# Retention attention followed by top-1 expert routing: a third buffer for transposed keys, and the gate weights by one transfer and eight copies

## The chip, the cores and the metric

The kernel runs on one core of a Trainium2 chip. The metric is the time of one execution on the device in microseconds (us), as the median of several runs. The engines named here are TensorE (PE; its weight loads are listed apart as PEld), VectorE (DVE), ScalarE (ACT), GpSimd (POOL) and SyncE (SP), which only issues transfers. Each works through its own instructions in order and waits on semaphores for the others. SBUF is the memory on the chip that they share, PSUM the one that TensorE writes its results to.

## The reference

Attention of the retention kind (a decay in place of a softmax) over 8 batches, 8 heads, 576 positions and heads of 64, and then a layer of 8 experts in which each of the 4608 tokens goes to the one expert with the highest logit.

```python
def _attn_ref(q, k, v):                       # each (8, 8, 576, 64)
    scores = scale * np.matmul(q, k.transpose(0, 1, 3, 2))
    gamma = 1.0 - 2.0 ** (-5.0 - np.arange(H))
    Dmat = np.where(rel >= 0, gamma[:, None, None] ** rel[None, :, :], 0.0)   # rel = i - j
    return np.matmul(scores * Dmat[None], v)

def _moe_ref(x, w_gate, w1, w2):              # x (4608, 512), w_gate (512, 8), w1 (8, 512, 1024), w2 (8, 1024, 512)
    logits = x @ w_gate
    expert_idx = np.argmax(logits, axis=1)
    ...                                       # softmax of the logits; gate_w = the winner's share
    for e in range(E):
        mask = expert_idx == e
        ye = np.maximum(x[mask] @ w1[e], 0.0) @ w2[e]
        out[mask] = gate_w[mask, None] * ye
    return out
```

`x` is the attention's output with the heads side by side.

## The kernel before

Attention goes through 40 blocks: for each of 8 batches four blocks of 128 positions (c = 0 to 3) and a remainder of 64 (c = 4, so blocks 4, 9, 14, ...). Block i+1 finds a running state `se` of what came before it. Keys and queries are scaled on GpSimd by their share of the decay (`scale_k`, `scale_q`), transposed on TensorE (`stage_TK`, `stage_TQ`) and copied from PSUM by ScalarE into `kT` and `qT`. For a remainder the 64 queries and 64 keys share one tile, so its `kT` serves as queries too and is read until the end of its own iteration. Pools hand out a fixed number of buffers for each tag (`bufs`) in turn: a tile waits until all readers of the one that had its buffer are done.

```python
    wkp = p1.enter_context(tc.tile_pool(name="wk", bufs=2))
    wk3 = p1.enter_context(tc.tile_pool(name="wk3", bufs=3))
# ... cut ...
    def stage_TK(i):
        if i >= NB:
            return
        kk = kks[i]
        pst = psw.tile([P, 512], F32, tag="W", name="psk")
        for p in range(NP):
            tr(pst[:, p * P:(p + 1) * P], kk[:, 2 * p:2 * p + 2, :].rearrange("p h d -> p (h d)"), ident[:, :])
        kT = wkp.tile([P, NP, P], F32, tag="kT")
        mark["kT"] = nc.scalar.copy(out=kT[:, :, :].rearrange("p a t -> p (a t)"), in_=pst[:, :])
        kTs[i] = kT
# ... cut: stage_S adds a block's keys and values to the state ("pss"); stage_SC makes the scores ...
    def stage_SC(i):
        if i >= NB:
            return
        b, c = blocks[i]
        kT = kTs.pop(i)
        sc = wk1.tile([P, 2, NP, P], F32, tag="sc")
        scs[i] = sc
        if c < NCH:
            qT = qTs[b]
            for p in range(NP):
                for u in range(2):
                    for j in range(2):
                        r = slice(j * DH, (j + 1) * DH)
                        mm(pssc[u * DH:(u + 1) * DH, j, p * P + u * DH:(p + 1) * P], kT[r, p, u * DH:(u + 1) * DH],
                           qT[r, p, c * P + u * DH:(c + 1) * P], True, True)
            mark["sc"] = nc.vector.tensor_tensor(
                out=sc[:, :, :, :].rearrange("p j a i -> p (j a) i"),
                in0=pssc[:, :, :].rearrange("p j (a i) -> p (j a) i", i=P),
                in1=mask[:, :].unsqueeze(1).to_broadcast([P, 2 * NP, P]), op=ALU.mult)
        else:
            qTs[(b, "r")] = kT
# ... cut: the remainder's own scores; stage_AV multiplies scores by values into "psx" ...
    def stage_IN(i):

        b, c = blocks[i]
        if c < NCH:
            mark["xT"] = nc.vector.tensor_copy(
                out=xTs[b][:, c, :].rearrange("p (w t) -> p w t", w=2), in_=psx[:, :, 0:2 * P])
            xbs[i] = wkb.tile([P, 2, 2 * P], BF16, tag="xb", name="xb")
            nc.scalar.copy(out=xbs[i][:, :, :], in_=psx[:, :, 0:2 * P])
        else:
            # ... cut ...
            se, qT = sts.pop((b, c)), qTs.pop((b, "r"))
            # ... cut: matmuls into psx that read the remainder's kT (here qT) ...
            xo = wk1.tile([P, 256], F32, tag="xo", name="xo")
            nc.scalar.copy(out=xo[:, :], in_=psx[:, 1, 256:512])
            xTs[(b, "r")] = wk1.tile([P, 256], F32, tag="xTr", name="xTr")
            mark["xT"] = nc.vector.tensor_tensor(out=xTs[(b, "r")][:, :], in0=psx[:, 0, 256:512], in1=xo[:, :],
                                                 op=ALU.add)
            xbs[i] = wkb.tile([P, 256], BF16, tag="xb", name="xb")
            nc.scalar.copy(out=xbs[i][:, :], in_=xTs[(b, "r")][:, :])
```

Before the blocks begin, SyncE issues the first loads of queries, keys and values (`load_q`, `load_k`, `load_v`, up to block 4), and then the gate weights. These are wanted in a form that fits the transposed output: `wgp` has, for each pair of heads and two variants, 64 rows of one head above 64 of another, and 8 of 32 columns filled. Eight transfers bring the pieces. The first use of `wgp` is `stage_L1` of the first batch, in the iteration of block 5.

```python
    wgp = attc.tile([P, 2, NP, 32], F32, name="wgp")
    nc.vector.memset(wgp[:, :, :, :], 0.0)
    wg4 = moe_w_gate.rearrange("(a u d) e -> u d a e", u=4, d=DH)
    for j in range(2):
        for w in range(2):
            nc.sync.dma_start(out=wgp[j * DH:(j + 1) * DH, 0, 2 * w:2 * w + 2, 0:E], in_=wg4[(3 * w, 2 - w)[j]])
            nc.sync.dma_start(out=wgp[j * DH:(j + 1) * DH, 1, w:NP:2, 0:E], in_=wg4[2 * w + (j ^ w)])
```

The loop over the blocks: GpSimd scales ahead by three blocks, keys are transposed ahead by two, scores are made ahead by one, and key and value loads are issued six blocks ahead, each after a mark of the pace. The constants of the routing are made on GpSimd in the iteration of block 3.

```python
    scale_k(0, nc.vector)
    stage_TK(0)
    for p in range(NP):
        scale_q(0, p, nc.vector)
        stage_TQ(0, p)
    scale_k(1)
    scale_k(2)
    stage_TK(1)
    stage_SC(0)
    stage_S(0)
    load_k(5)
    load_v(5)
# ... cut ...
    for i, (b, c) in enumerate(blocks):
        if i == 3:
            make_routing()

        if c > 0 and b + 1 < B:
            scale_q(b + 1, c - 1)
        scale_k(i + 3)
        fetch(early.get(i, 0))
        load_k(i + 6, mark.get("sc"))
        stage_TK(i + 2)
        if c > 0 and b + 1 < B:
            stage_TQ(b + 1, c - 1)
        if c == 1 and b > 0:
            stage_L2(b - 1)
        if i > 1:
            stage_R(i - 2)
        if c in (1, 3) and b + 2 < B:
            load_q(b + 2, c // 2, mark.get("kT"))
        stage_S(i + 1)
        stage_AV(i)
        if c == 0 and b > 0:
            stage_L1(b - 1)
        stage_IN(i)
        stage_SC(i + 1)
        load_v(i + 6, mark.get("xT"))
        if (b, c) == (B // 2, 1):
            rf = route_first()
        if rf is not None:
            steps(rf, 1.9)
```

`stage_R` writes a block's output as rows for the expert layer, `stage_L1` and `stage_L2` make a batch's logits, `route_first` is the routing of the first half of the tokens, a few VectorE steps in each iteration from batch 4 on. After the loop come the experts: rows gathered by token, transposed, multiplied by w1, through the ReLU, by w2, scaled, and scattered to the output.

Of the kernel before, what the change touches and what calls it, by code (L numbers as in the profile page):

```python
# [14 lines left out]
F32 = mybir.dt.float32  # L15
# [4 lines left out]
P = 128  # L20
B, H, S, DH = 8, 8, 576, 64
DM = H * DH
E, F = 8, 1024
NP = H // 2
# [6 lines left out]
NPT = DM // P  # L31
# [10 lines left out]
def kernel(  # L42
# [10 lines left out]
    nc = tc.nc  # L53
# [8 lines left out]
    def tr(out, in_, identity):  # L62
        nc.tensor.transpose(out=out, in_=in_, identity=identity)  # L63
# [24 lines left out]
    wkp = p1.enter_context(tc.tile_pool(name="wk", bufs=2))  # L88
    wk3 = p1.enter_context(tc.tile_pool(name="wk3", bufs=3))
# [3 lines left out]
    attc = p1.enter_context(tc.tile_pool(name="attc", bufs=1))  # L93
# [9 lines left out]
    def load_q(b, g, dep=None):  # L103

        if g == 0:
            qts[b] = ldq.tile([P, H, NCH, DH], F32, tag="q", name="qt")
        hs = slice(g * NP, (g + 1) * NP)
        after(nc.sync.dma_start(out=qts[b][:, hs, :, :],
                                in_=q[b, hs, 0:NCH * P, :].rearrange("h (p s) d -> p h s d", p=P)), dep)
# [7 lines left out]
    def load_k(i, dep=None):  # L117
# [5 lines that stand above are left out]
            load_kv(kts, "k", k, i, dep)  # L123
            return
        kts[i] = ldk.tile([P, H, DH], F32, tag="k", name="kt")
        for u in range(2):
            after(nc.sync.dma_start(out=kts[i][u * REM:(u + 1) * REM, :, :],
                                    in_=(q, k)[u][b, :, NCH * P:S, :].rearrange("h p d -> p h d")), dep)
# [90 lines left out]

    wgp = attc.tile([P, 2, NP, 32], F32, name="wgp")  # L220
    nc.vector.memset(wgp[:, :, :, :], 0.0)
    wg4 = moe_w_gate.rearrange("(a u d) e -> u d a e", u=4, d=DH)
    for j in range(2):
        for w in range(2):
            nc.sync.dma_start(out=wgp[j * DH:(j + 1) * DH, 0, 2 * w:2 * w + 2, 0:E], in_=wg4[(3 * w, 2 - w)[j]])
            nc.sync.dma_start(out=wgp[j * DH:(j + 1) * DH, 1, w:NP:2, 0:E], in_=wg4[2 * w + (j ^ w)])


    wb = {}
# [18 lines left out]
    def scale_q(b, p, eng=nc.gpsimd):  # L248
        h0 = 2 * p
        qq = wkp.tile([P, NCH, P], F32, tag="qq")  # L250
        eng.tensor_tensor(  # L251
            out=qq[:, :, :].rearrange("p s (h d) -> p h s d", d=DH), in0=qts[b][:, h0:h0 + 2, :, :],
            in1=qg[:, 0:NCH, h0:h0 + 2].rearrange("p s h -> p h s").unsqueeze(3)
                .to_broadcast([P, 2, NCH, DH]), op=ALU.mult)
        qqs[(b, p)] = qq

    def scale_k(i, eng=nc.gpsimd):
        if i >= NB:
            return
        kk = wk3.tile([P, H, DH], F32, tag="kk")  # L260
        eng.tensor_tensor(out=kk[:, :, :], in0=kts.pop(i)[:, :, :],  # L261
                          in1=kg[:, blocks[i][1], :].unsqueeze(2).to_broadcast([P, H, DH]), op=ALU.mult)
        kks[i] = kk

    def stage_TQ(b, p):

        qq = qqs.pop((b, p))
        pst = psw.tile([P, 512], F32, tag="W", name="psq")
        for s_ in range(NCH):
            tr(pst[:, s_:512:NCH], qq[:, s_, :], ident[:, :])  # L270
        if b not in qTs:
            qTs[b] = wkp.tile([P, NP, 512], F32, tag="qT", name="qT")
        nc.scalar.copy(out=qTs[b][:, p, :], in_=pst[:, :])  # L273
# [5 lines that stand above are left out]
        pst = psw.tile([P, 512], F32, tag="W", name="psk")  # L279
        for p in range(NP):  # L280
            tr(pst[:, p * P:(p + 1) * P], kk[:, 2 * p:2 * p + 2, :].rearrange("p h d -> p (h d)"), ident[:, :])
        kT = wkp.tile([P, NP, P], F32, tag="kT")
        mark["kT"] = nc.scalar.copy(out=kT[:, :, :].rearrange("p a t -> p (a t)"), in_=pst[:, :])  # L283
        kTs[i] = kT

    def stage_S(i):
# [4 lines that stand above are left out]
        kk = kks.pop(i)  # L291
        if c == NCH:
# [3 lines that stand above are left out]
                h = 2 * p + j  # L296
                mm(pss[j * DH:(j + 1) * DH, p * DH:(p + 1) * DH], kk[:, h, :], vts[i][:, h, :],
                   c == 0 and p == 0, c == NCH - 1)
        se = wkp.tile([P, NP, DH], F32, tag="se")
        mark["se"] = nc.scalar.copy(out=se[:, :, :].rearrange("p a d -> p (a d)"), in_=pss[:, 0:NP * DH])  # L300
        sts[(b, c + 1)] = se
# [132 lines left out]
    def stage_L2(b):  # L434
        lt = lts.pop(b)
        ps2 = psw.tile([P, 512], F32, tag="W", name="psl2")
        tr(ps2[:, 0:P], lt[:, 0:P], ident[:, :])
        tr(ps2[0:DH, P:2 * P], lt[:, P:P + DH], ident[:, :])
        t0 = b * NCOL
        nc.vector.tensor_copy(out=lg[:, t0:t0 + NCH, :],  # L440
                              in_=ps2[:, 0:P].rearrange("p (c n) -> p c n", n=32)[:, :, 0:E])
        nc.vector.tensor_reduce(out=lg[0:DH, t0 + NCH, :],
                                in_=ps2[0:DH, P:2 * P].rearrange("p (c n) -> p n c", n=32)[:, 0:E, :],
                                axis=AX.X, op=ALU.add)
# [17 lines left out]
    def make_routing():  # L462

        nc.gpsimd.memset(lg[:, :, :], 0.0)
        nc.gpsimd.memset(su1[:, :], -1.0)
        nc.gpsimd.affine_select(out=su1[:, :], in_=su1[:, :], pattern=[[-1, P]], base=0, channel_multiplier=1,
                                compare_op=ALU.is_ge, fill=0.0)
        nc.gpsimd.memset(onesb[:, :], 1.0)
        nc.gpsimd.iota(iota_r[:, :], pattern=[[1, P]], base=0, channel_multiplier=0,
                       allow_small_or_imprecise_dtypes=True)  # L470
        nc.gpsimd.iota(rev[:, :], pattern=[[-1, E]], base=E, channel_multiplier=0,
                       allow_small_or_imprecise_dtypes=True)
        nc.gpsimd.memset(off[:, :], 0.0)
        nc.gpsimd.memset(off[REM:P, :].rearrange("p (b c) -> p b c", c=NCOL)[:, :, NCH:NCOL], 100.0)
        nc.gpsimd.memset(rst[:, :, :], 1.0)
        nc.gpsimd.memset(rst[:, :, 0:1], 0.0)
        nc.gpsimd.iota(hi[:, :], pattern=[[S // 64, B], [2, NCOL]], base=0, channel_multiplier=0,
                       allow_small_or_imprecise_dtypes=True)
        nc.gpsimd.iota(lo[:, :], pattern=[[1, 1]], base=1, channel_multiplier=1,
                       allow_small_or_imprecise_dtypes=True)  # L480
        nc.gpsimd.tensor_copy(out=fld[:, :, 0], in_=hi[:, :])
        nc.gpsimd.tensor_copy(out=fld[:, :, 1], in_=lo[:, :].to_broadcast([P, NT]))
# [225 lines left out]
# [5 lines that stand above are left out]
# [13 lines left out]
    def fetch(n):  # L726
        for e, j in [wq.pop(0) for _ in range(min(n, len(wq)))]:
            load_w(e, j, 4, wpool if e < EW else wpool2)

    rf = None  # L730
    for i, (b, c) in enumerate(blocks):
        if i == 3:
            make_routing()

        if c > 0 and b + 1 < B:
# [24 lines that stand above are left out]
# [105 lines left out]
    with tc.If(over > 0):  # L865
        with ExitStack() as p3:
# [24 lines left out]
            for e in range(E):  # L891
# [4 lines left out]
                with tc.For_i(0, NT, 1) as t:  # L896
# [8 lines left out]
                        out=xg[:, :], out_offset=None, in_=x_rows[:, :],  # L905
# [16 lines left out]
                    for fb in range(NFB):  # L922
# [5 lines left out]
                        out=out[:, :], out_offset=bass.IndirectOffsetOnAxis(ap=ci[:, 0:1], axis=0),  # L928
                        in_=ys[:, :], in_offset=None, bounds_check=NTOK - 1, oob_is_err=False)
# [30 lines left out]
```

## Time and profile before

The time is 375.44 us (median of 3 runs, 374.24 to 375.72). The profiled execution has a span of 377.9 us.

| engine | busy, us | share of the span | instructions |
|---|---|---|---|
| TensorE (PE) | 325.7 | 86% | 4642 |
| its weight loads (PEld) | 240.3 | 64% | 4642 |
| VectorE (DVE) | 148.3 | 39% | 324 |
| ScalarE (ACT) | 167.6 | 44% | 373 |
| GpSimd (POOL) | 198.1 | 52% | 240 |

| stretch, us | what runs | TensorE busy, us | DMA share | GB/s |
|---|---|---|---|---|
| 40.7 to 62.6 | one batch of blocks | 20.10 of 21.90 | 0.80 | 191 |
| 62.6 to 84.5 | the next batch | 20.10 of 21.90 | 0.86 | 201 |
| 84.5 to 106.4 | the next batch | 20.10 of 21.90 | 0.88 | 203 |
| 177.0 to 204.0 | the last blocks, routing beside them | 22.24 of 27.00 | 1.07 | 196 |
| 204.0 to 245.0 | into the experts | 36.10 of 41.00 | 0.68 | 146 |
| 245.0 to 365.0 | the experts | 118.33 of 120.00 | 0.70 | 157 |

In the lines of a timeline the first two numbers are the start and the duration in microseconds, then come the engine (SPq is SyncE's queue), the line of the kernel, the operation, and what it writes and reads. "x8" is the number of instructions merged into the line. The brackets at the end hold how long the engine had been idle before it, and what ended that idle time. In a page's rows of digits each digit is a fortieth of the span: for an engine its busy share in tenths, for the clock the part of full speed that TensorE was granted. An engine that is idle costs time only when it is the one that the others wait for.

### The profile page before, as it was taken

The numbers are of one execution on the slowest core, as the hardware profiler recorded it, in microseconds if no ns is written. First come the engines' busy times: TensorE is split into PE (matmuls) and PEld (weight loads), VectorE is DVE, ScalarE is ACT, GpSimd is POOL, SyncE is SP. The second block draws the span as 40 slices with busy tenths as digits, with TensorE's granted clock in tenths as the row PEclk, the third lists the DMA queues.
The fourth block names the chain that finished last, engine by engine and source line by source line (L and its number), as shares of the span: only waits on it lengthen the run. The fifth ranks groups of instructions, "written<-read, shape, count | busy, mean of one in ns | idle before, by whom it ended". The sixth has DMA issues, their size and how long they took to land.

```text
span 377.9 us, 11155 instructions
## 1 busy us (share of the span) xinstructions
PE 325.7 (86%) x4642; PEld 240.3 (64%) x4642; DVE 148.3 (39%) x324; ACT 167.6 (44%) x373; POOL 198.1 (52%) x240
## 2 busy tenths in 40 slices
PE   2994899898989887996996899799999899999950
PEld 2774787786878676775785677355556466656520
DVE  5440243444426589443694396101122121212120
ACT  2451445456545535443444453355543536363500
POOL 2427452434545234298670165687767788754230
PEclk9997999999999999999699999999999999999995
DMA  7949879699888968869999398367998999933120
GB/s 195 238 96 252 192 181 209 162 222 211 205 206 213 208 161 194 206 167 211 215 158 218 98 161 185 99 148 160 210 194 139 208 192 208 232 110 111 59 73 7
DMA packets 113339, 65.34 MB, mean 173 GB/s; under 512 B 84094, under 2 KB 105598, under 8 KB 113280
## 3 DMA queue, kind: packets, MB, share of 16 engines
q0 software_dynamic: 18432, 31.47, 39.8%
q1 hardware_dynamic: 94848, 33.07, 37.3%
q8 instruction: 38, 0.62, 0.7%
q14 instruction: 21, 0.17, 0.2%
HBM read 67.14 MB, written 15.20 MB: 218 GB/s over the span
## 4 chain that ended last, share of the span: by engine, by line
PE 38%; issue 3%; POOL 3%; DVE 2%; ACT 2%; another core or an unknown queue 1%; DMA 1%; POOLq 0%; DVEq 0%; ACTq 0%
PE pm L60 16%; PE py L60 15%; PE psx L60 2%; PE pt L63 2%; POOL out_dram L799 1%; PE pssc L60 1%; DMA xg<-x_rows,tidg 1%; DVE sc L318 1%; PE psl L60 1%; POOL w1b L239 1%; PE pss L60 1%; POOL w2b L239 1%; DVE ys L798 1%; ACT ht L704 0%
## 5 line engine op out<-in xcount | busy, mean ns | idle before, releaser
L261 POOL TENSOR_TENSOR kk<-kt,kg 128x512 f32<-128x512 f32 x39 | 40.9, 1048 | 90.3 <-PE pss L60 56.0
L60 PE MATMUL pm<-xt,w1b 128*128 128x256 bf16 (+1 forms) x512 | 74.3, 303 | 2.9 <-ACT xt L689 2.9
L60 PE MATMUL py<-w2b,ht 128*128 128x512 bf16 x320 | 74.8, 379 | 1.6 <-ACT ht L704 1.6
L704 ACT ACTIVATE ht<-pm 128x384 bf16<-128x384 f32 (+1 forms) x96 | 50.5, 526 | 56.0 <-PE pm L60 43.8
L798 DVE TENSOR_SCALAR ys<-py,gat 128x512 f32<-128x512 f32 x40 | 29.9, 750 | 111.7 <-PE py L60 96.1
L799 POOL DMA_INDIRECT out_dram<-ys,tids x40 | 41.3, 1032 | 56.9 <-DVE ys L798 32.3
L60 PEld LDWEIGHTS <-w1b 128*128 128x128 bf16 x512 | 50.5, 99 | 26.2 <-issue 5.2
L60 PEld LDWEIGHTS <-ht 128*128 128x128 bf16 x320 | 29.9, 98 | 31.9 <-ACT ht L704 1.7
L647 POOL DMA_INDIRECT xg<-x_rows,tidg x40 | 41.1, 1028 | 15.9 <-issue 10.8
L60 PE MATMUL psx<-sc,vt 128*64 128x128 f32 (+1 forms) x640 | 39.2, 272 | 11.3 <-DVE sc L318 9.0
L60 PE MATMUL pssc<-qT,kT 64*64 64x128 f32 (+1 forms) x1024 | 38.5, 259 | 4.6 <-ACT qT L273 3.6
L318 DVE TENSOR_TENSOR sc<-pssc,mask 128x1024 f32<-128x1024 f32 x32 | 39.0, 1220 | 6.3 <-PE pssc L60 4.5
L363 DVE COPY xT<-psx 128x512 f32<-128x512 f32 x32 | 22.3, 695 | 48.4 <-PE psx L60 41.7
L366 ACT CAST xb<-psx 128x512 bf16<-128x512 f32 x32 | 18.7, 585 | 49.3 <-DVE xT L363 37.9
L60 PEld LDWEIGHTS psx<-sc,vt 128*64 128x64 f32 (+1 forms) x640 | 31.4, 140 | 14.1 <-ACT kT L283 10.9
L60 PEld LDWEIGHTS pssc<-qT,kT 64*64 64x64 f32 x1024 | 30.1, 138 | 8.6 <-ACT qT L273 5.4
L63 PE MATMUL psk<-ident,kk 128*128 128x128 f32 x160 | 27.6, 298 | 8.7 <-DVE kk L261 5.9
L283 ACT COPY kT<-psk 128x512 f32<-128x512 f32 x40 | 23.4, 585 | 22.8 <-PE psx L60 13.5
L689 ACT COPY xt<-pt 128x512 bf16<-128x512 bf16 x40 | 22.9, 585 | 22.3 <-PE pt L63 18.2
L251 POOL TENSOR_TENSOR qq<-qt,qg 128x512 f32<-128x512 f32 x28 | 29.8, 1066 | 0.2
L63 PE MATMUL psq<-ident,qq 128*128 128x128 f32 x128 | 22.0, 302 | 6.9 <-POOL qq L251 5.3
L63 PEld LDWEIGHTS psk<-ident,kk 128*128 128x128 f32 x160 | 18.1, 148 | 14.1 <-issue 9.0
(124 smaller groups left out, 366.5 us busy)
## 6 DMA issues: line engine op xcount, KB each, us to landing
kt<-in_k_dram SPq DMA_DIRECT2D x32, 256.0 KB, 4.8
qt<-in_q_dram SPq DMA_DIRECT2D x16, 512.0 KB, 7.0
vt<-in_v_dram SPq DMA_DIRECT2D x32, 256.0 KB, 4.7
w1b<-in_moe_w_dram POOLq DMA_DIRECT2D x32, 256.0 KB
w2b<-in_moe_w_dram POOLq DMA_DIRECT2D x32, 256.0 KB
x_rows<-xr SPq DMA_DIRECT2D x32, 128.0 KB, 5.8
kt<-in_q_dram SPq DMA_DIRECT2D x8, 128.0 KB, 4.3
kt<-in_k_dram SPq DMA_DIRECT2D x8, 128.0 KB, 4.4
```

The lines of the kernel that those rows point to most:

```text
L60: nc.tensor.matmul(out=out, lhsT=lhsT, rhs=rhs, start=start, stop=stop, skip_group_check=True)
L63: nc.tensor.transpose(out=out, in_=in_, identity=identity)
L251: eng.tensor_tensor(out=qq[:, :, :].rearrange("p s (h d) -> p h s d", d=DH), in0=qts[b][:, h0:h0 + 2, :, :], in1=qg[:, 0:NCH, h0:h0 + 2].r ...
L261: eng.tensor_tensor(out=kk[:, :, :], in0=kts.pop(i)[:, :, :], in1=kg[:, blocks[i][1], :].unsqueeze(2).to_broadcast([P, H, DH]), op=ALU.mult)
L283: mark["kT"] = nc.scalar.copy(out=kT[:, :, :].rearrange("p a t -> p (a t)"), in_=pst[:, :])
L318: mark["sc"] = nc.vector.tensor_tensor(out=sc[:, :, :, :].rearrange("p j a i -> p (j a) i"), in0=pssc[:, :, :].rearrange("p j (a i) -> p ( ...
L363: mark["xT"] = nc.vector.tensor_copy(out=xTs[b][:, c, :].rearrange("p (w t) -> p w t", w=2), in_=psx[:, :, 0:2 * P])
L647: nc.gpsimd.indirect_dma_start(out=xg[:, :], out_offset=None, in_=x_rows[0:nr, :], in_offset=bass.IndirectOffsetOnAxis(ap=slots[ph][1][:, ...
L689: nc.scalar.copy(out=xts[(e, ph)][:, :, j * P:(j + 1) * P], in_=pt[:, :, :])
L704: nc.scalar.activation(out=ht[:, f0:f0 + per, :], in_=pm[:, :, :], func=AF.Relu)
L798: nc.vector.tensor_scalar(out=ys[:, :], in0=py[:, :], scalar1=gat[:, i:i + 1], scalar2=None, op0=ALU.mult)
L799: nc.gpsimd.indirect_dma_start(out=next(outs)[:, :], out_offset=bass.IndirectOffsetOnAxis(ap=tids[:, i:i + 1], axis=0), in_=ys[:, :], in_o ...
```

## The change

Three things. The tile `kT` comes from a pool of three buffers instead of two, so that the copy of a block's transposed keys need not wait for the readers of the block two before it. The gate weights come in one transfer of 16 KB, issued by ScalarE, into a plain tile `wgn`, and eight copies on GpSimd spread them into `wgp`, from iteration 3 on; SyncE's eight transfers of 4 KB fall away, and with them their place ahead of the load of key block 5. The routing constants move from the iteration of block 3 to that of block 5, to leave the place on GpSimd to the copies.

```diff
--- before.py
+++ after.py
@@ -219,11 +219,19 @@
 
     wgp = attc.tile([P, 2, NP, 32], F32, name="wgp")
     nc.vector.memset(wgp[:, :, :, :], 0.0)
-    wg4 = moe_w_gate.rearrange("(a u d) e -> u d a e", u=4, d=DH)
-    for j in range(2):
-        for w in range(2):
-            nc.sync.dma_start(out=wgp[j * DH:(j + 1) * DH, 0, 2 * w:2 * w + 2, 0:E], in_=wg4[(3 * w, 2 - w)[j]])
-            nc.sync.dma_start(out=wgp[j * DH:(j + 1) * DH, 1, w:NP:2, 0:E], in_=wg4[2 * w + (j ^ w)])
+    wgn = attc.tile([P, NPT, E], F32, name="wgn")
+    nc.scalar.dma_start(out=wgn[:, :, :], in_=moe_w_gate.rearrange("(c p) e -> p c e", p=P))
+
+    def make_gate():
+        def put(j, dst, h0):
+
+            o = h0 % 2 * DH
+            nc.gpsimd.tensor_copy(out=dst[j * DH:(j + 1) * DH], in_=wgn[o:o + DH, h0 // 2:NPT:2, :])
+
+        for j in range(2):
+            for w in range(2):
+                put(j, wgp[:, 0, 2 * w:2 * w + 2, 0:E], (3 * w, 2 - w)[j])
+                put(j, wgp[:, 1, w:NP:2, 0:E], 2 * w + (j ^ w))
 
 
     wb = {}
@@ -279,7 +287,7 @@
         pst = psw.tile([P, 512], F32, tag="W", name="psk")
         for p in range(NP):
             tr(pst[:, p * P:(p + 1) * P], kk[:, 2 * p:2 * p + 2, :].rearrange("p h d -> p (h d)"), ident[:, :])
-        kT = wkp.tile([P, NP, P], F32, tag="kT")
+        kT = wk3.tile([P, NP, P], F32, tag="kT")
         mark["kT"] = nc.scalar.copy(out=kT[:, :, :].rearrange("p a t -> p (a t)"), in_=pst[:, :])
         kTs[i] = kT
 
@@ -730,6 +738,8 @@
     rf = None
     for i, (b, c) in enumerate(blocks):
         if i == 3:
+            make_gate()
+        if i == 5:
             make_routing()
 
         if c > 0 and b + 1 < B:
```

## The prediction

> **What bounds the kernel now.** I read the page first, then busy time by windows of 2 us, the timeline of two stretches, the waits, and the chain that ended last. From the page, TensorE's busy tenths and its granted clock, in 40 slices of 9.4 us:
>
> ```profile
> PE   2994899898989887996996899799999899999950
> ...
> PEclk9997999999999999999699999999999999999995
> ```
>
> TensorE is the engine to watch: nearly full almost everywhere. Two clock digits fall out of line, a 7 in slice 4 (28 to 38 us) and a 6 in slice 20 (179 to 189 us). In the windows, the columns are the length, the busy time (and count) of TensorE, its weight loads, VectorE, ScalarE and GpSimd, then the clock, the DMA share and GB/s:
>
> ```profile
> 18.00:20.00 2.00, 2.00 (x44) 1.71 (x40) 1.40 (x2) 0.69 (x2) 0.27 (x1) 1.00 1.02 270
> 20.00:22.00 2.00, 2.00 (x47) 1.67 (x48) 0.52 (x1) 0.96 (x2) 1.83 (x2) 1.00 0.44 87
> 22.00:24.00 2.00, 2.00 (x56) 1.83 (x46) 1.39 (x2) 1.05 (x3) 0.23 (x1) 1.00 0.16 19
> 24.00:26.00 2.00, 2.00 (x43) 1.71 (x45) 0.53 (x1) 1.53 (x4) 0.00 (x0) 1.00 0.07 4
> ...
> 28.00:30.00 2.00, 0.00 (x0) 0.00 (x0) 0.73 (x1) 0.01 (x1) 0.92 (x1) 1.00 1.21 243
> ...
> 34.00:36.00 2.00, 2.00 (x16) 1.74 (x17) 0.00 (x0) 1.08 (x3) 2.00 (x3) 0.50 1.31 256
> ```
>
> The DMA engines run dry between 20 and 26 us (87, 19, 4 GB/s against 270 just before), then TensorE is empty for 2 us, and from about 33 us it works at half clock. The timeline (start, duration, engine, line) says what SyncE did meanwhile:
>
> ```profile
> 18.31 0.59 SPq L225 DMA_DIRECT2D wgp<-in_moe_w_gate_dram  x1
> ...
> 24.73 0.61 SPq L226 DMA_DIRECT2D wgp<-in_moe_w_gate_dram  x1
> ...
> 25.43 0.54 SPq L114 DMA_DIRECT2D kt<-in_k_dram  x1
> ...
> 29.08 1.04 POOL L261 TENSOR_TENSOR kk<-kt,kg 128x512 f32<-128x512 f32 x1 [6.84 <-DMA kt<-in_k_dram]
> ...
> 30.17 0.65 PE L63 MATMUL psk<-ident,kk 128*128 128x128 f32 x4 [2.74 <-POOL kk L261]
> ```
>
> The eight gate-weight issues sit from 18.31 to 25.43 us ahead of the load of key block 5; GpSimd waits 6.84 us for that load and TensorE waits for GpSimd. The second stretch is the end of a batch (block 9 is a remainder of 64 rows, and its iteration makes the keys of block 11 ready):
>
> ```profile
> 63.46 0.58 ACT L283 COPY kT<-psk 128x512 f32<-128x512 f32 x1 [1.39 <-PE psx L60]
> ...
> 64.59 0.44 PE L60 MATMUL pssc<-qT,kT 64*64 64x128 f32 x8 [0.60 <-ACT qT L273]
> ...
> 65.21 0.43 ACT L386 COPY xo<-psx 128x256 f32<-128x256 f32 x1
> ...
> 65.68 0.42 DVE L388 TENSOR_TENSOR xTr<-psx,xo 128x256 f32<-128x256 f32 x1 [3.90 <-ACT xo L386]
> 66.02 1.21 DVE L318 TENSOR_TENSOR sc<-pssc,mask 128x1024 f32<-128x1024 f32 x1
> ...
> 67.38 1.09 PE L60 MATMUL psx<-sc,vt 128*64 128x128 f32 x16 [0.93 <-DVE sc L318]
> ```
>
> The copy into kT waits for matmuls (psx) that do not produce its input: they are the last readers of the remainder's kT, which holds the other of two buffers. ScalarE works in order, so qT, xr, se and xo queue behind it, then VectorE's xTr and sc. TensorE stands 0.60 + 0.93 = 1.53 us. The batches starting at 40.7, 62.6 and 84.5 us take 21.90 us each with 20.1 us of TensorE work, so this is most of what a batch loses. After 244 us the chain that ended last is almost only TensorE matmuls.
>
> **What the Trainium skill says.** "TensorE: Matmul & The Clock Gate", Part 1 (the HAM clock gate): the array runs at half rate after an idle window of some 3.4 us and at full rate again after a busy one. The trace agrees in kind: 0.50 follows the two idle stretches of 2.74 and 2.94 us around 30 us. "DMA: Bandwidth & Descriptors", Rules for kernel authors: coalesce many small transfers. Same page, Issuing engines are not separate DMA queues: another issuing engine saves only the time to issue. Here the issue time is the cost: 0.6 us or more each, while 4 KB lands in a median of 3.0 us. "Perfetto Trace Analysis", Optimization Strategy: the same gap repeating can mean too little room for the next tile. The 1.53 us per batch is such a gap.
>
> **The change, part by part.** (a) Eight SyncE issues go. The load of key block 5 moves from 25.43 to about 18.3 us. The DMA engines still drain until about 20.5 us, so its 256 KB land near 22 us and GpSimd scales them by about 23.3 us, well before TensorE asks at 27.4 us. The following loads move up the same way: at 240 GB/s 256 KB take 1.1 us, and a block of 4.2 us needs about 0.85 MB or 3.5 us, so the stream holds. The iteration of block 3 ran from 27.43 (end of pssc) to 38.64 us (next psk). The same iteration one batch later, block 8, runs from 57.42 to 60.78, 3.36 us. So the next psk comes at 27.43 + 3.36 = 30.79 instead of 38.64: 7.85 us. The half clock lasts a little into the next group (0.92 instead of 0.66 us), giving 0.26 more. **Sum 8.1 us**, on the path, because TensorE has no slack in the stretches after it.
>
> (b) Added: one issue on ScalarE near 2.7 us, when that engine is idle until 7.07, and a transfer of 512 pieces of 32 bytes among the first loads, when the start does wait for DMA. The eight transfers, twice as many pieces, cost in the windows 22 to 26 us (0.16 + 0.07) x 2 us = 0.5 us of all engines, perhaps three quarters of them; so one half of the whole is about 0.3 us. I charge **0.3 us**.
>
> (c) Added: eight GpSimd copies of 64 x 16 elements. The copies of 64 x 64 (tri) take about 0.25 us each, so at most 2 us, in block 3's iteration. There GpSimd would have the keys of block 5 at about 23.3 us, the gate copies to 25.3, qq to 26.4, kk to 27.4; TensorE asks for that qq at about 28.1. Hidden. Routing constants (29.9 to 32.7 us now, 2.7 us) move to block 5's iteration, where GpSimd otherwise waits for a kk buffer (5.79 us at the same place one batch later): hidden too, and the 2.94 us wait for qq at 33.8 us, part of (a), is not replaced.
>
> (d) A third kT buffer. ScalarE is free at 61.97 us after xb and psk is done at 61.44, so kT starts 1.49 us sooner, and with the spacings of the trace xo starts at 63.71 instead of 65.21; xTr follows at +0.47, sc at +0.34 = 64.52, while pssc, no longer held, ends at 64.4. TensorE restarts 1.36 us after the start of sc: 65.88 instead of 67.38. So 1.5 us per batch with a plain remainder. Seven remainders copy kT while the old buffer is held (seven waits, 13.5 us). In four (blocks 4, 9, 14, 19) the gain is about 1.45 us, in the fifth the two gaps are 0.60 + 0.81, so 1.35; in the sixth 0.60 + 0.23, so 0.8; in the seventh, at 183 us and at half clock, I take 0.9. Sum 5.8 + 1.35 + 0.8 + 0.9 = **8.85 us**.
>
> Total 8.1 + 8.85 - 0.3 = 16.65 us. 375.44 - 16.65 = 358.8; I say 359.
>
> **The rivals.** First: the gain is given back downstream. Between 159 and 180 us GpSimd is nearly full with gathers, weight loads, qq and kk, and TensorE waits 2.37 us for qq at 179.7; between 177 and 204 us the DMA share is 1.07. If these ran at a time of their own, up to the last three remainders and some of (a) would vanish, perhaps 5 to 8 us, so 364 to 367. Against it: the gathers start when routing is done on VectorE, routing is paced by blocks, and so the whole stretch moves with TensorE. Second: DMA becomes the bound. At 40.7 to 106.4 us its share is 0.80 to 0.88; batches of 20.4 instead of 21.9 us push it to 0.86 to 0.95. If block loads then arrived late, (d) would bring half: about 363. Against it: after 29 us GpSimd never again waits for a key load in this trace, and it waits 5.79 us per batch for matmuls instead, which is slack. Third: the tiny pieces delay the first query and key loads, or the gate copies arrive late and hold qq with another half clock: 2 to 7 us back, 361 to 366. For it: the start is bound by DMA (1.5 us wait for q, 0.93 for keys). Against it: 16 KB in all. A slower kernel would need something none of these shows.
>
> **Range and chances.** 2% is 7.5 us. Either main part alone reaches about that, and the rivals take at most half of the sum, so faster by over 2%: 0.92, within 2%: 0.07, slower: 0.01. The range is 354.5 (downstream waits of 2.2 us shrink too, fewer half-clock stretches) to 365 (one rival holds).
>
> **What would show it.** In the profile after: no dry DMA windows at 20 to 26 us, block 5's kk done by about 24 us, psk near 27.4 us, and clock 1.00 from 28 to 40 us (a); ScalarE's kT no longer waiting for psx, batches of about 20.4 us instead of 21.9 (d); the stretch from the half-clock dip near 165 us to the end as long as before, within 2 us. Wrong would be: a kk waiting for DMA in mid-kernel, GpSimd's wait before psq at the dip grown by what was saved, a first psk later by over 1 us, or a half clock still at 30 us.

## The result and the profile after

The changed kernel takes 358.76 us (median of 4 runs, 356.46 to 361.23), the kernel before 374.84 us beside it (median of 4, 373.78 to 375.72). The ratio is 0.957, with a 95% interval of 0.950 to 0.964: faster by 16.1 us. The profiled execution has a span of 354.6 us. The profile of before, 377.9 us, was of an execution slower than that kernel's median and this one is of an execution faster than its own, so the two profiles lie 23.3 us apart, 7 us more than the medians. What belongs to the profiles alone is named where it comes up.

The page of the changed kernel, TensorE's busy tenths and its granted clock in 40 slices:

```profile
PE   3898999999998987978878999999999999999940
...
PEclk9999999999999999998999999999999999999995
```

The 7 in slice 4 of the clock is gone, and of the 6 in slice 20 an 8 in slice 19 is left. The same stretch in windows of 2 us (columns as before: length, TensorE, weight loads, VectorE, ScalarE, GpSimd, then clock, DMA share, GB/s):

```profile
20.00:22.00 2.00, 2.00 (x59) 1.66 (x56) 0.69 (x1) 0.44 (x2) 1.86 (x2) 1.00 1.09 264
22.00:24.00 2.00, 2.00 (x36) 1.89 (x38) 1.23 (x1) 1.95 (x5) 0.39 (x2) 1.00 1.32 225
24.00:26.00 2.00, 2.00 (x62) 1.73 (x56) 0.58 (x1) 0.56 (x2) 1.87 (x8) 1.00 1.04 195
...
28.00:30.00 2.00, 2.00 (x50) 1.71 (x52) 0.00 (x0) 1.14 (x3) 2.00 (x3) 1.00 0.97 300
...
34.00:36.00 2.00, 1.50 (x26) 1.32 (x25) 1.20 (x2) 0.95 (x3) 1.07 (x2) 1.00 0.85 124
```

Where the DMA engines moved 87, 19 and 4 GB/s they now move 264, 225 and 195; TensorE is busy in 28 to 30 us, where it was empty, and stays at full clock. The timeline of the same place:

```profile
18.85 0.55 SPq L114 DMA_DIRECT2D kt<-in_k_dram  x1
...
23.80 1.04 POOL L269 TENSOR_TENSOR kk<-kt,kg 128x512 f32<-128x512 f32 x1 [1.61 <-DMA kt<-in_k_dram]
...
24.79 1.54 POOL L229 COPY wgp<-wgn 64x16 f32<-64x16 f32 x8
...
26.08 0.66 PE L63 MATMUL psk<-ident,kk 128*128 128x128 f32 x4
...
27.52 0.66 PE L63 MATMUL psq<-ident,qq 128*128 128x128 f32 x4 [0.78 <-POOL qq L259]
```

The load of block 5's keys is issued at 18.85 us instead of 25.43, they are scaled from 23.80 us instead of 29.08, and psk no longer waits. The eight gate copies take 1.54 us right behind them, and the next psq now waits 0.78 us for a qq that came after the copies. The remainder of the second batch, block 9, in the timeline:

```profile
52.99 0.59 ACT L291 COPY kT<-psk 128x512 f32<-128x512 f32 x1
...
54.18 1.05 PE L60 MATMUL pssc<-qT,kT 64*64 64x128 f32 x32
...
54.73 0.45 ACT L394 COPY xo<-psx 128x256 f32<-128x256 f32 x1
...
55.21 0.42 DVE L396 TENSOR_TENSOR xTr<-psx,xo 128x256 f32<-128x256 f32 x1 [2.41 <-ACT xo L394]
55.55 1.22 DVE L326 TENSOR_TENSOR sc<-pssc,mask 128x1024 f32<-128x1024 f32 x1
...
56.91 1.09 PE L60 MATMUL psx<-sc,vt 128*64 128x128 f32 x16 [0.26 <-DVE sc L326]
```

The copy into kT no longer has a wait in brackets, the 32 pssc matmuls run in one piece, and of 0.60 + 0.93 us of TensorE's idle time 0.26 is left. The two batches from 53.66 to 94.46 us, each counted from the first psx<-sc,vt of its remainder to that of the next, take 20.40 us each (before 21.90), with 19.88 us of TensorE work. The batch ahead of them takes 21.62, with a pause of 0.89 us that the last section takes up. One number went up, in GpSimd's waits:

```profile
POOL kk L269 <- PE pss L60: 45.5, 13, 6.8
...
POOL kk L269 <- DMA kt<-in_k_dram: 19.1, 8, 6.2
```

(columns: microseconds in all, times, longest.) GpSimd waits for key loads 19.1 us in 8 waits where it was 9.7 us in 3. As long as TensorE does not wait for GpSimd in turn, this costs nothing.

### The profile page after: what moved, and what is told of

It is laid out like the page before. It is cut to its first block, busy times and chain, and to the rows that moved or that the text cites. A ratio compares the mean times of both kernels' runs of the same rounds, so it can differ in the third digit from the quotient of the medians.

```text
span 354.6 us, 11148 instructions
## 1 busy us (share of the span) xinstructions
PE 316.2 (89%) x4642; PEld 235.7 (66%) x4642; DVE 149.9 (42%) x324; ACT 167.6 (47%) x373; POOL 199.2 (56%) x248
## 4 chain that ended last, share of the span: by engine, by line
PE 43%; POOL 4%; issue 4%; DVE 4%; DMA 1%; ACT 1%; POOLq 0%; DVEq 0%
PE py L60 17%; PE pm L60 17%; PE psx L60 3%; PE pt L63 2%; POOL out_dram L809 1%; PE pssc L60 1%; DMA xg<-x_rows,tidg 1%; POOL xg L655 1%; POOL w2b L247 1%; DVE sc L326 1%; PE psl L60 1%; POOL w1b L247 1%; DVE ys L808 1%; DVE pos L576 1%; PE pss L60 1%
## 5 line engine op out<-in xcount | busy, mean ns | idle before, releaser
L60 PE MATMUL pm<-xt,w1b 128*128 128x256 bf16 (+1 forms) x512 | 72.6, 300 | 0.5 <-ACT xt L697 0.5
L60 PE MATMUL pssc<-qT,kT 64*64 64x128 f32 (+1 forms) x1024 | 34.3, 251 | 0.9 <-issue 0.9
L697 ACT COPY xt<-pt 128x512 bf16<-128x512 bf16 x40 | 22.8, 586 | 21.7 <-PE pt L63 21.7
L60 PEld LDWEIGHTS pssc<-qT,kT 64*64 64x64 f32 x1024 | 28.5, 133 | 2.2 <-issue 1.6
L247 POOL DMA_DIRECT2D w2b<-in_moe_w_dram x32 | 24.2, 778 | 2.9 <-DMA w2b<-in_moe_w_dram 2.9
```

Of the source, the lines that this page charges most:

```text
L60: nc.tensor.matmul(out=out, lhsT=lhsT, rhs=rhs, start=start, stop=stop, skip_group_check=True)
L247: after(nc.gpsimd.dma_start(out=wb[e][part // n][:, o:o + m, :], in_=w[e, o * P:(o + m) * P, :].rearrange("(c p) f -> p c f", p=P)), dep)
L697: nc.scalar.copy(out=xts[(e, ph)][:, :, j * P:(j + 1) * P], in_=pt[:, :, :])
```

## The experiments

In what follows a landmark is used: the start of a block's first psx<-sc,vt matmul in the timeline, called its AV. Each time stands beside runs of the kernel before on the same chip; a ratio is to those, and is of mean times, so that it can differ a little from the quotient of the medians. A saving in microseconds is worked out from the ratio; where two variants shared a chip and only their medians are compared, the text says so. One execution each of the last two variants was in a slower state that comes with any kernel, and is left out of their medians.

**The third kT buffer alone.** The kernel before with one line changed:

```diff
-        kT = wkp.tile([P, NP, P], F32, tag="kT")
+        kT = wk3.tile([P, NP, P], F32, tag="kT")
```

> The kernel before with only the third kT buffer. Theory of the prediction (two separate gains, 8.85 us for the buffer): 374.8 - 8.85 = 366 us, batches of 20.4 instead of 21.9 us, ScalarE's kT no longer waiting for psx; the dry DMA windows, the empty 2 us and the half clock near 30 us stay. Rival (the gain of the changed kernel comes from the start alone, and what a batch saves is given back on GpSimd or by DMA later): 372 to 375 us.

Measured: 363.49 us, ratio 0.973 (0.970 to 0.976) to 373.55 us, so 10.1 us less. The dry DMA stretch and the half clock stand as in the kernel before, as its windows show:

```profile
24.00:26.00 2.00, 1.30 (x48) 1.05 (x40) 1.32 (x2) 0.96 (x2) 0.00 (x0) 1.00 0.14 16
...
30.00:32.00 2.00, 0.00 (x0) 0.00 (x0) 0.00 (x0) 0.59 (x1) 1.83 (x13) 0.56 1.32 213
32.00:34.00 2.00, 1.10 (x6) 1.03 (x7) 0.00 (x0) 0.00 (x0) 2.00 (x3) 0.50 1.12 315
```

The buffer is worth its gain by itself.

**The gate part alone.** The changed kernel with kT back in the pool of two:

```diff
-        kT = wk3.tile([P, NP, P], F32, tag="kT")
+        kT = wkp.tile([P, NP, P], F32, tag="kT")
```

> The changed kernel with kT back in two buffers, so only the gate weights' new way and the later routing constants. Theory: 8.1 - 0.3 us gained, 374.8 - 7.8 = 367 us, psk of block 6 near 30.5 instead of 38.6 us, then batches of 21.9 us with gaps of 0.60 and 0.93 us. Rival (the two parts help each other or cover the same wait): clearly more than 370 or less than 364 us. A side question: the first pssc came at 11.6 us in the changed kernel and at 13.6 us before; if the new place in the queues does that, it is about 11.6 here, if it is chance, it scatters.

Measured: 367.03 us, ratio 0.983 (0.978 to 0.988), so 6.4 us less than before. The two parts, 10.1 and 6.4, add up to 16.5; the whole change measured 16.1. With their intervals the parts are 9.0 to 11.2 and 4.7 to 8.1 us. The batches have 21.9 us again. Late in the attention phase TensorE's timeline shows the gaps of the two-buffer kernel once more, beside a wait for GpSimd:

```profile
172.19 1.12 PE L63 MATMUL psq<-ident,qq 128*128 128x128 f32 x4 [2.78 <-POOL qq L259]
176.89 0.44 PE L60 MATMUL pssc<-qT,kT 64*64 64x128 f32 x8 [0.60 <-ACT qT L281]
179.68 1.09 PE L60 MATMUL psx<-sc,vt 128*64 128x128 f32 x16 [0.93 <-DVE sc L326]
```

After the 2.78 us the clock was 0.50 and 0.69 in the two windows from 172 to 176 us (the psq group takes 1.12 us instead of 0.66).

**The one transfer from SyncE instead of ScalarE.**

```diff
-    nc.scalar.dma_start(out=wgn[:, :, :], in_=...)
+    nc.sync.dma_start(out=wgn[:, :, :], in_=...)
```

> The changed kernel with its one gate transfer issued by SyncE in the old place instead of ScalarE. Theory (eight issues in front of key block 5 were the cost, not the engine that issues): one issue costs 0.6 us in the queue, and key block 5 is scaled about 1.3 us before TensorE asks, so within 1 us of the changed kernel, 359 us. Rival (the other engine, or the early landing, is what pays): slower by 3 us or more, 362 to 366 us.

Measured: 357.98 us, ratio 0.957 (0.954 to 0.961), the changed kernel's own. Which engine issues the one transfer makes no difference that the runs resolve, nor does the time of its issue: here it stands in the old place, at 18.79 us. In this profile block 5's keys came later, and the copies behind them:

```profile
24.65 1.04 POOL L269 TENSOR_TENSOR kk<-kt,kg 128x512 f32<-128x512 f32 x1 [2.81 <-DMA kt<-in_k_dram]
25.64 1.54 POOL L229 COPY wgp<-wgn 64x16 f32<-64x16 f32 x8
...
28.38 1.02 PE L63 MATMUL psq<-ident,qq 128*128 128x128 f32 x4 [1.97 <-POOL qq L259]
```

The 1.97 us brought half clock back for a while (0.63 and 0.52 in 28 to 32 us), and AV of block 4 stands at 34.5 instead of 32.0 us.

**The eight issues put back.** The changed kernel, plus the eight old transfers into a tile wgx that nothing reads:

```diff
+    wgx = attc.tile([P, 2, NP, 32], F32, name="wgx")
+    nc.vector.memset(wgx[:, :, :, :], 0.0)
+    wg4 = moe_w_gate.rearrange("(a u d) e -> u d a e", u=4, d=DH)
+    for j in range(2):
+        for w in range(2):
+            nc.sync.dma_start(out=wgx[...], in_=wg4[...])   # two of these, as in the kernel before
```

> The changed kernel with the eight old transfers issued by SyncE in the old place as well, into a tile that nothing reads. Theory (their time in SyncE's queue is the cost): the dry DMA windows, the wait for key block 5 and the half clock come back, 7 to 8 us of loss, 366 us. Rival (what cost the time before was the routing constants on GpSimd ahead of qq, which stay moved here): within 2 us of the changed kernel, 359 to 361 us.

Measured: 365.05 us, ratio 0.976 (0.971 to 0.981): 9.0 of the 16.1 us are left, 7 us are lost. The timeline has the old stall back, without the old routing constants in its place:

```profile
19.55 0.60 SPq L227 DMA_DIRECT2D wgx<-in_moe_w_gate_dram  x1
...
25.21 0.61 SPq L228 DMA_DIRECT2D wgx<-in_moe_w_gate_dram  x1
25.92 0.54 SPq L114 DMA_DIRECT2D kt<-in_k_dram  x1
...
29.64 1.04 POOL L276 TENSOR_TENSOR kk<-kt,kg 128x512 f32<-128x512 f32 x1 [7.34 <-DMA kt<-in_k_dram]
30.74 1.12 PE L63 MATMUL psk<-ident,kk 128*128 128x128 f32 x4 [4.54 <-POOL kk L276]
```

The eight issues hold the load of block 5 until 25.92 us, GpSimd waits 7.34 us for it, and TensorE 4.54. DMA moves 15 and 4 GB/s in 22 to 26 us, so it is not the transfers' own traffic that delays the load. The place in the queue is the cost. The same eight issues placed behind the load were not run.

**The routing constants back in block 3's iteration**, beside the copies:

```diff
         if i == 3:
             make_gate()
-        if i == 5:
             make_routing()
```

> The changed kernel with the routing constants back in iteration 3, after the gate copies. Theory (the two causes of the old loss add up: the queue, and 2.7 us of constants ahead of qq): TensorE waits 0.8 + 2.7 = 3.5 us for qq at block 3 and runs at half clock after it, which cost about 2 us before; 4 to 5.5 us more than the changed kernel, 363 to 364 us. Rival (the issues in SyncE's queue were the whole loss): 359 us.

Measured: 362.08 us, ratio 0.967 (0.965 to 0.970), 3.2 us more by the medians than the next variant, with which it shared a chip. The timeline:

```profile
27.43 0.36 POOL L472 MEMSET lg<- 128x320 f32 x1
...
30.02 1.06 POOL L259 TENSOR_TENSOR qq<-qt,qg 128x512 f32<-128x512 f32 x1
...
31.14 1.12 PE L63 MATMUL psq<-ident,qq 128*128 128x128 f32 x4 [3.90 <-POOL qq L259]
...
36.00 1.12 PE L63 MATMUL psk<-ident,kk 128*128 128x128 f32 x4
```

From 27.43 us the constants stand ahead of qq on GpSimd; TensorE waits 3.90 us and then works at half clock (1.12 us for a group of 0.66). So moving them was needed: the queue alone would have uncovered this wait.

**The copies moved to block 5's iteration as well.**

```diff
-        if i == 3:
-            make_gate()
         if i == 5:
+            make_gate()
             make_routing()
```

> The changed kernel with the gate copies in iteration 5, just ahead of the routing constants, where GpSimd has waited for a kk buffer, instead of iteration 3. Theory (the copies, 1.54 us, stand ahead of qq and held TensorE 0.78 us at block 3 in the changed kernel's profile): 0.8 us less, about 358 us, psq of block 3 without a wait for qq, the first psx of block 4 near 31.3 us. Rival (hidden, as the prediction said): 358.8 us as before, the same psq.

Measured: 358.89 us, ratio 0.959 (0.956 to 0.961). The wait of 0.78 us ahead of psq is gone in the profile (psq at 27.13 us), and the time is not below the changed kernel's. The saving is too small to be seen against what else varies.

**The copies made twice**, as a dose of the same suspicion:

```diff
         if i == 3:
             make_gate()
+            make_gate()
```

> The changed kernel with its eight gate copies made twice, in iteration 3. Theory (they stand on the path): the wait for qq at block 3 grows from 0.78 to 2.3 us, and the half clock may follow, 1.5 to 4 us more, 360 to 363 us. Rival (hidden): 359 us.

Measured: 358.53 us, ratio 0.959 (0.957 to 0.962). In the timeline the wait is 2.29 us, 1.51 more than in the changed kernel's profile; the second set of copies takes 1.73 (3.27 instead of 1.54):

```profile
24.77 3.27 POOL L229 COPY wgp<-wgn 64x16 f32<-64x16 f32 x16
...
28.12 1.06 POOL L259 TENSOR_TENSOR qq<-qt,qg 128x512 f32<-128x512 f32 x1
...
29.23 0.66 PE L63 MATMUL psq<-ident,qq 128*128 128x128 f32 x4 [2.29 <-POOL qq L259]
```

In the time it can't be told from the variant without a wait. The two together bound the copies' cost: in the profiles they do hold TensorE, in the time it is less than the runs resolve.

**A fourth kT buffer.**

```diff
-        kT = wk3.tile([P, NP, P], F32, tag="kT")
+        kT = wk4.tile([P, NP, P], F32, tag="kT")
```

> The changed kernel with four kT buffers instead of three. Theory (a copy had to wait only for the block two before it, and with three buffers no kT waits for psx any more): no change, 358 to 360 us. Rival (the ring is still short at a remainder): 1 us or more less.

Measured: 359.94 us, ratio 0.962 (0.959 to 0.965): nothing gained; the intervals overlap with the changed kernel's. Three buffers are enough.

**An attempt at a further gain: weight loads spread.** The changed kernel still has TensorE wait 1.86 and 1.22 us for qq at 158 and 164 us, where GpSimd issues weight loads beside gathers.

```diff
-    early = {i: 1 for i in range(12, NB - 8, 4)} | {i: 2 for i in range(NB - 8, NB)}
+    early = {i: 1 for i in range(10, NB - 8, 2)} | {i: 2 for i in range(NB - 5, NB)}
```

> The changed kernel, with the 21 weight loads that run beside the attention spread otherwise: one in every second iteration from block 10 to block 30 and two in each of the last five, instead of one in every fourth from block 12 and two in each of the last eight. Theory (TensorE waits for GpSimd at 158 and 164 us, 1.86 and 1.22 us in the profile of the changed kernel, because GpSimd issues weight loads there beside gathers): those two waits go, the last plain AV (block 39) starts 2 to 3 us before 185.3, and the time is 2 to 3 us below the changed kernel run beside it, about 356 us. Rival (the DMA engines, at a share of 0.91 to 0.99 per batch, are the limit as soon as anything is added): the batches from 93 us on become longer than 20.40 us by 0.3 us or more each and the time is that of the changed kernel or 1 to 2 us above it. Rival (the gathers alone fill GpSimd): waits and time unchanged within 1 us.

Measured: 361.81 us, ratio 0.958 (0.952 to 0.964), not to be told from the changed kernel beside it (0.959). Both waits are gone, and in the profile the stretch from AV of block 30 to AV of block 35 takes 22.9 us instead of 26.1 in the run of the changed kernel beside it. From 25 to 30 it takes 23.0 instead of 25.1, but there the other run was at half clock for 3.41 us; the changed kernel's first profile, at full clock, took 23.6. From 10 to 15 it is 21.7 instead of 20.4 us, and from 20 to 25 24.8 instead of 21.9: 4.3 of the 5.2 us are lost ahead of it, and the experts after it took 1.3 us more, as much as one wait of 1.31 us for ScalarE's ht at 276.6 us, behind a "remote" releaser. Of the 4.3 us, 1.33 and 0.82 are pauses of TensorE with no releaser, which the last section takes up. The timeline of GpSimd and TensorE in the longer of these stretches:

```profile
100.39 1.04 POOL L269 TENSOR_TENSOR kk<-kt,kg 128x512 f32<-128x512 f32 x1 [6.76 <-DMA kt<-in_k_dram]
...
115.58 1.09 PE L60 MATMUL psx<-sc,vt 128*64 128x128 f32 x16 [2.90 <-DVE sc L326]
```

GpSimd waits for key loads 49.1 us in 23 waits in the whole profile (22.1 in 9 in the run beside it), and DMA's share in 93.2 to 113.6 us is 1.08 instead of 0.99: the loads come late. But TensorE's wait of 2.90 us is for VectorE (1.68 beside it), so that the late loads cost the time was not shown. What follows is only that these two waits for GpSimd can't be had for nothing.

**The changed kernel again**, on that same chip, unaltered.

> The changed kernel itself, unaltered, beside the version with the spread weight loads, so that differences of one or two microseconds can be told from a difference of chips. Theory: 358 to 359.5 us, a ratio to the kernel before of 0.956 to 0.960, and in the profile batches of 20.40 us, with waits before psq near 158 and 164 us. If the pauses of TensorE for which the profile names no releaser (0.89 us at 34.5 us in the first profile of this kernel) belong to the kernel, they come again at the same place; if they are chance, they are elsewhere or absent.

Measured: 360.15 us, ratio 0.959 (0.953 to 0.964) to a median of 377.26 us. This chip is a little slower for both kernels. Its timeline at the gate copies:

```profile
27.48 0.66 PE L63 MATMUL psq<-ident,qq 128*128 128x128 f32 x4 [0.37 <-POOL qq L259]
```

The wait behind the copies is 0.37 us here and was 0.78 in the first profile of the same kernel. The three batches from 32.00 to 93.26 us take 20.39 to 20.47 us, and ahead of psq at 164.24 us it waits 2.21 us; near 158 us it has no such wait.

## Why the prediction was right, point by point

The sum was 16.65 us less, 359 us; measured were 16.1 us less, 358.76. The mechanisms were as predicted but for one: the gate copies were not hidden. Measured alone, one main term comes out smaller than predicted and the other larger, so part of the closeness of the sum looks like luck. The times alone do not settle it: 7.8 us lies within the 4.7 to 8.1 of the one, 8.85 just below the 9.0 to 11.2 of the other. The profiles show the two misjudged steps.

| term | predicted | measured alone |
|---|---|---|
| (a), (b), (c): gate issues, transfer, copies, constants | -8.1 + 0.3 + 0 = -7.8 us | -6.4 us (gate part alone); 7.0 us lost with the eight issues back |
| (d): third kT buffer | -8.85 us | -10.1 us (buffer alone) |
| sum | -16.65 us | -16.1 us |

**(a), the queue.** Right in its chain: dry DMA windows gone, kk of block 5 done at 24.84 us ("by about 24"; the working had 23.3), clock 1.00 from 28 to 40 us. psk itself came at 26.08 us, 1.3 us ahead of the predicted place. That shift was there before the gate transfers could act: in the profile of before the first AV is at 17.1 us, in all eleven others at 13.7 to 14.5, at 13.7 in that of the buffer alone, whose start is the old one. So the slow start belonged to that one execution. From first AV to the AV of block 4 the buffer-alone profile takes 25.6 us, the changed kernel 17.7 and, run again, 18.3: 7.3 to 7.9 us, near the 8.1 of the working.

The step that failed in these parts is (c), "Hidden". The working put the copies' end at 25.3 us and qq ready before TensorE asks at about 28.1; it placed the question in the clock time of a profile with a late start, and took the load of block 5 to land near 22 us, some 3.7 us after its issue. In the changed kernel's profile the issue is at 18.85 us and kk starts only at 23.80, 4.95 us later; the copies end at 26.33. TensorE asked at 26.7 us, and the wait for qq was 0.37 us (again), 0.78 (first), 0.81 (gate alone), 0.93 (weights spread), 1.60 (fourth buffer) and 1.97 (from SyncE). It was long where the key load came late: kk starts at 23.80 us in the first, at 24.65 in the SyncE and at 25.44 in the fourth-buffer profile. In eight profiles without the old issues and with the constants moved, AV of block 4 lies at 31.7 to 32.2 us five times and at 33.7 to 34.5 three times (copies twice among them), mean 32.7; with the old issues and the third buffer 39.3 and 39.8. The difference of the means, 6.8 us, is near what the times show (6.4 and 7.0); the five early ones alone would give 7.6, the case that the working took. That is rival three in a mild form.

**Two causes in one term.** (a) held two things apart only by name: the place in the queue, and the routing constants. Each alone brings a stall and a half clock back: 7.0 us for the queue, 3.2 to 3.6 us for the constants (medians on one chip), more together than the gate part is worth. They do not add up, since each hides a part of the other: with the queue in place, taking the constants away shortens the wait for qq only from 2.93 us (buffer alone) to 1.51 (eight issues back); without the queue they lengthen it to 3.90.

**(b), the transfer.** 0.3 us was charged. The first AV is at 13.7 us in the profile with the eight transfers and the third buffer, and at 13.7 to 14.5 in those with one; a cost of 0.3 us can neither be seen nor excluded.

**(d), the buffer.** The path was as worked out (1.5 us per plain batch, 21.90 to 20.40). Lengths from AV to AV in microseconds show where its sum was short:

| stretch, by AV of block | before | buffer alone | gate alone | changed | changed again |
|---|---|---|---|---|---|
| 4 to 25 | 93.4 | 86.0 | 93.3 | 87.5 | 86.4 |
| 25 to 30 | 24.3 | 25.2 | 25.8 | 23.6 | 25.1 |
| 30 to 35 | 29.0 | 25.2 | 28.8 | 26.3 | 26.1 |
| 35 to 39 | 15.9 | 16.0 | 15.9 | 15.9 | 16.1 |
| at half clock, 25 to 30 | 0 | 3.41 | 3.41 | 0 | 3.41 |
| at half clock, 30 to 35 | 6.83 | 0 | 3.41 | 3.41 | 0 |

The first row holds five of the seven remainders: predicted 4 x 1.45 + 1.35 = 7.15 us, measured 93.4 - 86.0 = 7.3 (from the unrounded 93.37 and 86.03) in one pair, 93.4 - 86.4 = 7.0 in another (87.5 holds a pause of 0.9, below). The sixth, "0.8", shows between profiles of the same clock: 24.3 - 23.6 = 0.7 at full clock, 25.8 - 25.1 = 0.7 with 3.41 us at half clock, which itself costs 1.5 to 1.6 us there. The term of (d) that was mis-sized is the seventh, "at half clock, I take 0.9": the two-buffer kernels take 28.8 and 29.0 us, the three-buffer ones 25.2 to 26.3, 2.5 to 3.8 us less. Where the clock is back at full by then, as in the gate-alone profile, the gaps are 0.60 + 0.93 us and not 0.9 together. Most of the rest is half clock: buffer-alone had none of it in this stretch, gate-alone 3.41 us and before 6.83. The third buffer does not prevent it, as the changed kernel's first profile has 3.41 us of it there, from 158.28 us, which is the 8 left in its clock digits. Gate-alone waited 2.78 us for qq and fell to 0.50, buffer-alone waited 2.77 us and stayed at 1.00. The Trainium skill, "TensorE: Matmul & The Clock Gate", Part 1, says the activity window is free-running, so that the same kernel can meet it in different phases. The clock records agree: 2.43 us of the one wait lie within one window of 3.41 us, and the other is split, 1.70 and 1.07 us, between two. So in these profiles part of what three buffers gained beyond the gaps is a matter of phase; the last section has the working.

**Rival one**, given back downstream: no. AV of block 39 is 18.0 us earlier in the changed profile (203.31 to 185.31), the first expert transposes 18.0 (204.17 to 186.18); the waits for qq near 160 us moved with TensorE. The further 5.3 us by which the two profiles differ up to the end came in the experts, where the profile of before has two waits of ScalarE, 2.3 us ahead of xt and 2.2 ahead of ht, whose releaser it gives only as "remote"; TensorE waits 2.35 and 1.19 us behind them and is at half clock for 3.41 us. That belongs to the execution and not to the kernel: the changed kernel's second profile has TensorE wait 1.86 us for xt there too, while from the first pm matmul to the last matmul eight of the twelve profiles take 151.9 to 152.1 us and the buffer alone, with the old transfers, 153.1, against 157.5 in the profile of before. So the sign "as long as before, within 2 us" can't be read from this one pair.

**Rival two**, DMA as the bound: not in the changed kernel, as its batches of 20.40 us with 19.88 of TensorE work show, but near. Its share in stretches of 20.4 us from 32.0 us on is 0.92, 0.99, 0.91 and 1.02 (run again 0.97, 1.01, 0.85 and 0.99), and with the weight loads spread it is 1.08 in the fourth, where keys come late. The prediction's "wrong would be a kk waiting for DMA in mid-kernel" was the wrong sign to name: kk does wait (19.1 us in 8 waits), while psk waits for it once, 0.88 us at 17.31.

## What to carry to other kernels

Look at what stands ahead of the first starved load in its queue: eight transfers of 4 KB cost no bandwidth that could be seen and 7 us in their place. A gap of the same length in every batch, ended by a copy that waits for readers of another buffer, is worth a buffer; count it per batch, and where other waits or a change of clock lie beside it, give the count a wide range, and compare profiles at equal clock. When a wait is removed, list what else becomes ready only then on the same in-order engine, and check the landmarks of a profile against its start before taking clock times from it.

## What the runs showed that was not expected

**A small issue can be the larger cost.** The Trainium skill, "DMA: Bandwidth & Descriptors", Issuing engines are not separate DMA queues, calls the issue time usually small relative to the transfer. Here an issue on SyncE took 0.60 us or more (five of 0.60, two of 0.61 and one of 1.73 in the run with eight put back), 6.3 us in a row for 32 KB, and that run lost 7 us; the engine of one single issue made no difference (357.98 against 358.76 us).

**Pauses of TensorE that nothing in the profile explains.** In the changed kernel, and twice with the copies moved to block 5:

```profile
34.50 0.27 PE L60 MATMUL pssc<-qT,kT 64*64 64x64 f32 x2 [0.89 <-issue]
```

```profile
34.97 0.27 PE L60 MATMUL pssc<-qT,kT 64*64 64x64 f32 x2 [1.54 <-issue]
...
118.85 1.09 PE L60 MATMUL pssc<-qT,kT 64*64 64x128 f32 x32 [1.75 <-issue]
```

"Issue" means that the profile shows nothing that TensorE waited for. Such pauses of 0.7 to 1.8 us came in six of the twelve profiles, once or twice each, in the changed kernel's first and not in its second. Counted in TensorE's matmuls they stand at five places of the program only: ahead of number 471 (twice), 1352, 1855, 1982 and 2233 (four times, each in another kernel), and these places lie 881, 503, 127 and 251 apart, each within 1 of a multiple of 126. The nine end 2.45 to 2.91 us after the start of a packet of the DMA queue that the page calls "q8 instruction" (38 packets of 16 KB), which shares the engines with the loads. Instructions fetched in pieces, a piece at times too late, would look so; but no run took the cause apart, and it stays open. Such pauses are as long as the differences that the smaller experiments asked for.

**Half clock goes by fixed windows, and a half-idle one is enough.** In each of the twelve profiles the stretches of half clock last 3.41 us or 6.83 us (longer only at the end, when TensorE is done), and their starts lie whole multiples of 3.413 us apart: in the buffer-alone profile at 30.25, 142.89 and 194.09 us, 33 and 15 windows apart. Laid on that grid, between 12 and 340 us, a window at full clock in which TensorE had been idle for 1.87 us or more was followed by half clock in all 18 cases, and one with less than 1.67 us in none; between these it came 6 times and stayed away 8 times. (Idle time is counted from the trace's matmul ends, which are modelled.) The prediction had taken an idle window of some 3.4 us; a little over half of one was enough here. So a wait of 2 us costs half clock when it falls within one window, and none when it is split between two: the 1.97 us of the SyncE run lie within one, and of the 2.29 us with copies made twice 0.58 and 1.71 in two.
